# Attention and a mixture of experts: GpSimd makes the low parts of the next rows, ScalarE scales a block's last half

## The chip, the cores and the metric

The program runs on one core of one Trainium2 chip. Its time is the device time of one execution in microseconds (us); lower is better. The times of the kernel before are those of three runs, with their median; one more execution was profiled. Engines are named as the profile names them: PE is TensorE, DVE is VectorE, ACT is ScalarE, POOL is GpSimd, SP is SyncE, which here issues transfers.

## What is computed

Attention with pooled keys and values gives x; then each token goes through one expert, picked by a gate that may keep the expert of the token before.

```python
attn = softmax(q @ mean8(k).T / sqrt(64)); x = attn @ mean8(v)      # B 8, H 8, S 576, head 64
logits = x @ w_gate                                                   # 8 experts
e[s]   = argmax(logits[s]) if s == 0 or sigmoid(x[s] @ w_local) < 0.5 else e[s-1]
out[s] = softmax(logits[s])[e[s]] * (relu(x[s] @ w1[e[s]]) @ w2[e[s]])    # 512 -> 1024 -> 512
```

## The kernel before, in words

Up to some 200 us the program computes the attention, routes the 4608 tokens and lists them by expert; that part is written as a plan of steps and is not touched here. What follows works on *blocks* of 256 listed rows (two halves of 128) that share one expert. The first blocks are in the plan; the rest is a loop at line 1197 over a table that the kernel itself has computed. With these inputs the loop makes 19 passes, one block each. A pass with two halves is a *full block*; a pass with one half only (`l1_one`) is a *single-half pass*.

Every product is made of three products of parts: a number is cut into a high part (rounded to the matmul's type, a copy on ACT) and a low part (the number less its high part, a subtract, on DVE). So x has `xt[:, :, 0]` and `xt[:, :, 1]`, the weights have `w1h` and `w1l`, `w2h` and `w2l`, the hidden values `ht_h` and `ht_l`.

One pass runs so, engine by engine in the order in which the code stands (the schedule is by hand; each engine keeps the order of the code and waits on semaphores):

- `head`: DVE takes the row numbers of the block after the next (`m_d`, `idk`); POOL gathers these rows from DRAM into `xg` (`fetch`, L1098 and L1099, then two indirect transfers, L299).
- Layer 1: in a full block eight block columns, each of four pairs of matmuls L322 and L324 (one pair for each quarter of the 512 inputs: `w1h` by both parts of x, then `w1l` by the high part) into one of six PSUM tiles. ACT copies a piece out (L329), DVE adds (L330), ACT makes `ht_h` (L334) and DVE `ht_l` (L335). In between DVE transposes the next block's rows, which SP had written out and read back in pieces (L303, L307), into `xs` (L310). A single-half pass has its own form (L976 to L991), in which DVE transposes all rows at once (L982) before it makes `ht_l` (L991).
- Layer 2 of half 1 (`l2(1)`, full blocks only). A half's layer 2 is 24 matmuls L346.
- `rest`: SP writes `xg` out and reads it back turned. If the next block has another expert (`chg > 0`, in six passes), ACT casts the four quarters of the loaded `raw1` to `w1h` (L172) and DVE subtracts for `w1l` (L173). DVE shifts the row numbers (`meta_shift`, L1165). Half 1 of the output is scaled by the gate (`emit_scale(1)`, L1078, DVE, from PSUM) and POOL scatters it to the output's rows (`emit_rows`, L1087 to L1089). `next_rows` cuts the next block's x into parts: two ACT casts (L315), two DVE subtracts (L316), each for two quarters. Then `l2(0)` on PE, the new `w2h` and `w2l` (L177, L178) where the expert changes, the scale of half 0 on DVE and its scatter on POOL. `seen_o` writes one number into a half of `ob` so that the next scale is ordered behind the scatter.

`ob`, `zf`, `m_e` and `m_a` are small tables and the output buffer of a block; `o_ps` are its two PSUM tiles, 2348 for half 1 and 2347 for half 0 in the listings below. Line 1243 is the end of the program, with barriers.

Of the kernel before, what the change touches and what calls it, by code (L numbers as in the profile page):

```python
# [8 lines left out]
F32 = mybir.dt.float32  # L9
F32R = mybir.dt.float32r  # L10
I32 = mybir.dt.int32
AF = mybir.ActivationFunctionType
ALU = mybir.AluOpType
# [92 lines left out]
def moe_attention(ctx: ExitStack, tc: tile.TileContext, q, q_st, k, v, v_st, w_gate, w1, w2, out):  # L106
    nc = tc.nc
# [133 lines left out]
    m_a = route.tile([P, 2, 2], F32, name="m_a", bufs=1)  # L241
# [39 lines left out]
    def rows_split(c2, tp, xt):  # L281
        cs = slice(2 * c2, 2 * c2 + 2)
        tv = tp.rearrange("p (c n) -> p c n", c=2)
        nc.scalar.copy(out=xt[:, cs, 0, :], in_=tv)
        nc.vector.tensor_tensor(out=xt[:, cs, 1, :], in0=tv, in1=xt[:, cs, 0, :].bitcast(F32), op=ALU.subtract)
# [5 lines left out]
    def row_numbers(out, m):  # L291
        nc.vector.tensor_copy(out=out, in_=m[:, :, 0])  # L292
# [9 lines left out]
    def rows_pieces():  # L302
        nc.sync.dma_start(xd.rearrange("(h p) d -> p h d", h=2), xg)  # L303

    def pieces_rows():
        for r in range(4):
            nc.sync.dma_start(xq[r * QP:(r + 1) * QP], xd[:, r * P:(r + 1) * P].rearrange("(m t) j -> t m j", t=QP))  # L307
# [4 lines left out]
    def next_rows():  # L312
        for c2 in range(2):
            cs = slice(2 * c2, 2 * c2 + 2)
            nc.scalar.copy(out=xt[:, cs, 0, :], in_=xs[:, cs, :])  # L315
            nc.vector.tensor_tensor(out=xt[:, cs, 1, :], in0=xs[:, cs, :], in1=xt[:, cs, 0, :].bitcast(F32), op=ALU.subtract)  # L316

    TERMS = ((0, 0), (0, 1), (1, 0))

# [18 lines left out]
    def l2(h, kks=range(KF), to=None):  # L338
        to = to or o_ps
        if len(kks) == 1:  # L340
            jobs = [(kk, i, j) for kk in kks for (i, j) in TERMS]
        else:
            jobs = [(kk, i, j) for k0 in range(0, KF, 4) for i in range(2) for kk in range(k0, k0 + 4) for j in range(2 - i)]
        n = 3 * kks[0]
        for (kk, i, j) in jobs:
            nc.tensor.matmul(out=to[h], lhsT=ht[i][:, kk, h * P:(h + 1) * P], rhs=W2[j][:, kk, :],  # L346
                             start=(n == 0), stop=(n == 3 * KF - 1))
            n += 1

    with ExitStack() as actx:  # L350
# [419 lines left out]
        def do(name, n):  # L770
# [136 lines left out]
            elif op == "i2":  # L907
                ids_load(bass.ds(entry(2, 1, (EN.SP,), NU32 - TB), TB))
            elif op == "ld":
                n0 = entry(0, 3, (EN.SP,), E - 1)  # L910
                load1(rw1, n0)
                load2(rl2, n0)
            elif op in ("e0", "e1"):
                h = int(op[1])
                emit_scale(h)
                if not h:
                    seen_o(1)
                apart(emit_rows(h))
            elif op == "f0":
                rows_meta(m_b, NS)  # L920
            elif op == "f1":
                ids_take(m_c)
                row_numbers(idf, m_c)
            elif op == "f2":
                xg = ld.tile([P, 2, D], F32, name="vt_in", bufs=3)
                xq = ld.tile([P, TB, P], F32, name="vt_in", bufs=3)
                xs = ld.tile([P, KD, 2 * P], F32, name="vt_in", bufs=3)
                xgs["f"] = ld.tile([P, 2, D], F32, name="qt", bufs=4)
                gather(xgs["f"], idf)
            elif op == "i3":  # L930
                ids_load(bass.ds(entry(3, 1, (EN.SP,), NU32 - TB), TB))
            else:
                raise ValueError(name)
# [10 lines left out]
        ob = sp.tile([P, 2, D], F32, name="ob")  # L944
# [14 lines left out]
        o_ps = [pp.tile([P, D], F32, name=f"o_ps{i}") for i in range(2)]  # L959
# [114 lines left out]
            nc.sync.dma_start(tab.rearrange("o (j c) -> o j c", c=TI), tabc[0:TROWS, :])  # L1074
            yield

        def emit_scale(h):
            nc.vector.tensor_scalar(out=ob[:, h, :], in0=o_ps[h], scalar1=m_a[:, h, 1:2], scalar2=None, op0=ALU.mult)  # L1078

        def seen_o(h):  # L1080
            nc.gpsimd.tensor_tensor(out=ob[:, h, 0:1], in0=zf1, in1=zf1, op=ALU.add)  # L1081
# [4 lines left out]
        def emit_rows(h):  # L1086
            nc.gpsimd.tensor_tensor(out=m_e[h], in0=m_i[:, h:h + 1], in1=zi, op=ALU.add)  # L1087
            nc.gpsimd.tensor_tensor(out=zf2[:, h:h + 1], in0=m_e[h].bitcast(F32), in1=ob[:, h, 0:1], op=ALU.mult)  # L1088
            return nc.gpsimd.indirect_dma_start(out=outv, out_offset=bass.IndirectOffsetOnAxis(ap=m_e[h][:, 0:1], axis=0),  # L1089
                                                in_=ob[:, h, :], in_offset=None, bounds_check=NT - 1, oob_is_err=False)  # L1090

        def meta_shift():
            nc.vector.tensor_copy(out=m_a, in_=m_b)
            row_numbers(m_i, m_b)
            nc.vector.tensor_copy(out=m_b, in_=m_c)
# [35 lines left out]
    def weights1(chg, nx):  # L1131
        for c in range(KD):
            split1(rw1(c), c, nc.vector)
        with tc.If(chg > 1):
            load1(rw1, nx)

    def weights2(chg, nx):
        for c in range(KF // 2):
            split2(rw2(c), c, nc.vector)
        with tc.If(chg > 1):  # L1140
            load2(rl2, nx)

    def changes(j):
        return entry(j + 1, 2, (EN.Activation, EN.DVE, EN.SP), 2), entry(j + 1, 3, (EN.SP,), E - 1)

    def first(chg, nx):
        with tc.If(chg > 0):
            weights1(chg, nx)
# [10 lines left out]
    def rest(j, turned=False):  # L1159
        rows_pieces()  # L1160
        pieces_rows()
        chg, nx = changes(j)
        first(chg, nx)
        meta_shift()
        nc.vector.tensor_copy(out=m_c, in_=m_d)  # L1165
        if turned:
            for c2 in range(2):
                rows_split(c2, hp[3 + c2], xt)
        seen_o(0)
        emit_scale(1)  # L1170
        first_half = emit_rows(1)
        if not turned:
            next_rows()
        l2(0)
        with tc.If(chg > 0):  # L1175
            weights2(chg, nx)
        emit_scale(0)
        tc.declare_no_dep(emit_rows(0).ins, first_half.ins, reason="rows of a block are distinct")
        seen_o(1)

# [11 lines left out]
    for c2 in range(2):  # L1192
        rows_turn(c2, xgs["f"], hp[3 + c2])
    rest(1, turned=True)
    trips = entry(0, 4, ALLE, NB2)
    man.close()
    with tc.For_i(2, trips, 1, iteration_sync="reg_based", name="blocks") as iv:  # L1197
        with tc.manual_schedule():
            two = entry(iv, 0, (EN.PE, EN.Activation, EN.DVE), 1)
            head(iv)  # L1200
            with tc.If(two > 0) as both:
                two_halves()
            with both.Else():
                l1_one()
            rest(iv)
# [41 lines left out]
```

## Time and profile before

| what | value |
|---|---|
| median of three runs | 626.25 us (622.35, 626.25, 628.47) |
| profiled execution | 623.03 us, span 621.3 us |
| PE busy, share of the span | 594.5 us, 96% |
| DVE / ACT / POOL busy | 439.7 / 291.8 / 273.6 us |
| mean granted clock of TensorE | 0.991 |
| transfers, share of 16 engines' span, SP's queue / POOL's queue | 43.5% / 11.0% |

The span runs from the first to the last instruction; the run's time is 1.7 us longer. Busy shares are means over the attention, the loop and the end, which have different limits, so the rows further down are read by stretch. Ends of matmuls are modelled, and spans on POOL are rough.

### The profile page before, as it was taken

The numbers are of one execution on the slowest core, as the hardware profiler recorded it, in microseconds if no ns is written. First come the engines' busy times: TensorE is split into PE (matmuls) and PEld (weight loads), VectorE is DVE, ScalarE is ACT, GpSimd is POOL, SyncE is SP. The second block draws the span as 40 slices with busy tenths as digits, with TensorE's granted clock in tenths as the row PEclk, the third lists the DMA queues.
The fourth block names the chain that finished last, engine by engine and source line by source line (L and its number), as shares of the span: only waits on it lengthen the run. The fifth ranks groups of instructions, "written<-read, shape, count | busy, mean of one in ns | idle before, by whom it ended". The sixth has DMA issues, their size and how long they took to land. (4 is left out here: it accounts for less than half of the span.)

```text
span 621.3 us, 14355 instructions
## 1 busy us (share of the span) xinstructions
PE 594.5 (96%) x3386; PEld 509.3 (82%) x3387; DVE 439.7 (71%) x1035; ACT 291.8 (47%) x697; POOL 273.6 (44%) x505
## 2 busy tenths in 40 slices
PE   8999999999999999999999999999999999999991
PEld 7898988898878878888887877787888888888870
DVE  7899898999766426565885686889556686654781
ACT  2777777965433313242742373746233363422550
POOL 6686776776673425134134326132352213341242
PEclk9999999999999999999999999999999999999996
DMA  8998973975003584331663486577543385322403
GB/s 340 356 383 303 365 276 103 318 173 204 19 2 102 176 301 135 102 118 68 211 228 113 143 259 219 186 242 267 196 127 105 101 258 195 115 71 85 118 27 99
DMA packets 62009, 111.95 MB, mean 180 GB/s; under 512 B 13466, under 2 KB 33946, under 8 KB 61980
## 3 DMA queue, kind: packets, MB, share of 16 engines
q1 hardware_dynamic: 53468, 89.54, 43.5%
q0 software_dynamic: 8512, 22.07, 11.0%
q8 instruction: 13, 0.21, 0.1%
q14 instruction: 16, 0.13, 0.1%
HBM read 81.88 MB, written 31.80 MB: 183 GB/s over the span
## 5 line engine op out<-in xcount | busy, mean ns | idle before, releaser
L322 PE MATMUL hp<-x,w1h 128*128 128x512 f32 x364 | 130.7, 400 | 2.5 <-DVE x L316 2.5
L346 PE MATMUL o_ps<-w2h,ht_h 128*128 128x512 f32 x312 | 122.8, 393 | 1.2 <-ACT ht_h L990 1.2
L346 PE MATMUL o_ps<-w2l,ht_h 128*128 128x512 f32 x312 | 122.1, 391 | 0.4 <-DVE w2l L178 0.2
L324 PE MATMUL hp<-x,w1l 128*128 128x256 f32 x364 | 102.2, 281 | 0.0
L329 ACT COPY hs<-hp 128x256 f32<-128x256 f32 x91 | 33.4, 369 | 125.8 <-PE hp L324 120.5
L346 PE MATMUL o_ps<-w2h,ht_l 128*128 128x512 f32 x312 | 87.8, 391 | 1.4 <-DVE ht_l L991 1.4
L322 PEld LDWEIGHTS hp<-x,w1h 128*128 128x128 f32 x364 | 68.4, 188 | 20.4 <-issue 3.8
L334 ACT ACTIVATE ht_h<-hs 128x256 fp32r<-128x256 f32 x136 | 57.1, 420 | 37.5 <-DVE hs L330 30.4
L1087 POOL TENSOR_TENSOR m_e<-m_i,zi 128x1 int32<-128x1 int32 x42 | 8.5, 201 | 142.3 <-DVE m_i L292 136.4
L346 PEld LDWEIGHTS o_ps<-w2h,ht_h 128*128 128x128 f32 x312 | 58.6, 188 | 14.6 <-issue 2.2
L346 PEld LDWEIGHTS o_ps<-w2h,ht_l 128*128 128x128 f32 x312 | 58.4, 188 | 14.5 <-DVE ht_l L991 2.2
L1078 DVE TENSOR_SCALAR ob<-o_ps,m_a 128x512 f32<-128x512 f32 x42 | 31.5, 750 | 53.9 <-PE o_ps L346 50.6
L324 PEld LDWEIGHTS hp<-x,w1l 128*128 128x128 f32 x364 | 68.9, 189 | 0.7
L346 PEld LDWEIGHTS o_ps<-w2l,ht_h 128*128 128x128 f32 x312 | 58.7, 188 | 12.5 <-DVE w2l L178 1.3
L565 PE MATMUL op<-vaug,aT 128*128 128x148 f32 (+4 forms) x448 | 66.0, 306 | 0.7 <-ACT osb L367 0.6
L565 PEld LDWEIGHTS op<-vaug,aT 128*128 128x128 f32 (+1 forms) x448 | 60.0, 179 | 3.9 <-issue 1.3
L335 DVE SCALAR_TENSOR_TENSOR ht_l<-hs,ht_h 128x256 fp32r<-128x256 f32 x136 | 56.4, 416 | 5.9 <-ACT ht_h L334 5.5
L1088 POOL TENSOR_TENSOR zf<-m_e,ob 128x1 f32<-128x1 f32 x42 | 13.9, 331 | 96.1 <-DVE ob L1078 65.2
L1089 POOL DMA_INDIRECT out<-ob,m_e x42 | 45.8, 1091 | 18.8 <-issue 18.8
L330 DVE TENSOR_TENSOR hs<-hp,hs 128x256 f32<-128x256 f32 x91 | 37.3, 417 | 19.9 <-ACT hs L329 11.5
L704 POOL DMA_INDIRECT ids<-pm,pos x36 | 38.7, 1076 | 17.0 <-DVE pos L699 8.0
L299 POOL DMA_INDIRECT vt_in<-x_rows,idk x40 | 39.8, 995 | 10.1 <-issue 8.1
(256 smaller groups left out, 1170.2 us busy)
## 6 DMA issues: line engine op xcount, KB each, us to landing
raw<-in_moe_w SPq DMA_DIRECT2D x48, 512.0 KB
xd<-vt_in SPq DMA_DIRECT2D x20, 512.0 KB
vt_in<-xd SPq DMA_DIRECT2D x80, 128.0 KB
kk<-in_k SPq DMA_DIRECT2D x16, 576.0 KB
qt<-in_q SPq DMA_DIRECT2D x16, 512.0 KB
vt_in<-in_v SPq DMA_DIRECT2D x16, 512.0 KB
x_rows<-xs SPq DMA_DIRECT2D x16, 512.0 KB
vt_in<-in_v_st SPq DMA_DIRECT2D x8, 256.0 KB
```

Source lines behind the costliest of these rows:

```text
L299: nc.gpsimd.indirect_dma_start(out=xg[:, h, :], out_offset=None, in_=x_rows[0:NT + 1], in_offset=bass.IndirectOffsetOnAxis(ap=idk[:, h:h + ...
L322: nc.tensor.matmul(out=ps, lhsT=W1[0][:, kk, f * P:(f + 1) * P], rhs=xt[:, kk].rearrange("p i n -> p (i n)"), start=(kk == 0), stop=False, ...
L324: nc.tensor.matmul(out=ps[:, 0:2 * P], lhsT=W1[1][:, kk, f * P:(f + 1) * P], rhs=xt[:, kk, 0, :], start=False, stop=(kk == KD - 1), skip_g ...
L329: nc.scalar.copy(out=hb[:, 0, :], in_=ps[:, 2 * P:])
L330: nc.vector.tensor_tensor(out=hb[:, 1, :], in0=ps[:, 0:2 * P], in1=hb[:, 0, :], op=ALU.add)
L334: nc.scalar.activation(out=ht[0][:, f, :], in_=hb, func=AF.Relu)
L335: nc.vector.scalar_tensor_tensor(out=ht[1][:, f, :], in0=hb, scalar=0.0, in1=ht[0][:, f, :].bitcast(F32), op0=ALU.max, op1=ALU.subtract)
L346: nc.tensor.matmul(out=to[h], lhsT=ht[i][:, kk, h * P:(h + 1) * P], rhs=W2[j][:, kk, :], start=(n == 0), stop=(n == 3 * KF - 1))
L565: nc.tensor.matmul(out=out, lhsT=lhs, rhs=rhs if len(out.shape) == 3 else rhs.rearrange("p s x -> p (s x)"), start=all(x[0] != n for x in ...
L704: ins = nc.gpsimd.indirect_dma_start(out=ids.rearrange("t m w -> (t m) w"), out_offset=bass.IndirectOffsetOnAxis(ap=pos[:, u:u + 1], axis= ...
L1078: nc.vector.tensor_scalar(out=ob[:, h, :], in0=o_ps[h], scalar1=m_a[:, h, 1:2], scalar2=None, op0=ALU.mult)
L1089: return nc.gpsimd.indirect_dma_start(out=outv, out_offset=bass.IndirectOffsetOnAxis(ap=m_e[h][:, 0:1], axis=0), in_=ob[:, h, :], in_offse ...
```

## The change

Two edits, both in what `rest` issues. The low parts of the next rows (L316) are made by POOL instead of DVE, in each call of `next_rows`; and `next_rows` is called earlier, ahead of `meta_shift` and of the first scatter's work on POOL. The scale of half 0 is made by ACT (an activation that copies with a scale), behind the `w2h` casts, instead of by DVE; the scale of half 1 stays on DVE, and so do both scales of the first block, in the plan. The block ahead of the loop (`turned`) takes its x by another way and changes only in its last scale. Lines from 1078 on stand 1 to 3 lower in the kernel after.

```diff
--- before.py
+++ after.py
@@ -313,7 +313,7 @@
         for c2 in range(2):
             cs = slice(2 * c2, 2 * c2 + 2)
             nc.scalar.copy(out=xt[:, cs, 0, :], in_=xs[:, cs, :])
-            nc.vector.tensor_tensor(out=xt[:, cs, 1, :], in0=xs[:, cs, :], in1=xt[:, cs, 0, :].bitcast(F32), op=ALU.subtract)
+            nc.gpsimd.tensor_tensor(out=xt[:, cs, 1, :], in0=xs[:, cs, :], in1=xt[:, cs, 0, :].bitcast(F32), op=ALU.subtract)
 
     TERMS = ((0, 0), (0, 1), (1, 0))
 
@@ -1074,7 +1074,10 @@
             nc.sync.dma_start(tab.rearrange("o (j c) -> o j c", c=TI), tabc[0:TROWS, :])
             yield
 
-        def emit_scale(h):
+        def emit_scale(h, late=False):
+            if late:
+                nc.scalar.activation(out=ob[:, h, :], in_=o_ps[h], func=AF.Copy, scale=m_a[:, h, 1:2])
+                return
             nc.vector.tensor_scalar(out=ob[:, h, :], in0=o_ps[h], scalar1=m_a[:, h, 1:2], scalar2=None, op0=ALU.mult)
 
         def seen_o(h):
@@ -1161,6 +1164,8 @@
         pieces_rows()
         chg, nx = changes(j)
         first(chg, nx)
+        if not turned:
+            next_rows()
         meta_shift()
         nc.vector.tensor_copy(out=m_c, in_=m_d)
         if turned:
@@ -1169,12 +1174,10 @@
         seen_o(0)
         emit_scale(1)
         first_half = emit_rows(1)
-        if not turned:
-            next_rows()
         l2(0)
         with tc.If(chg > 0):
             weights2(chg, nx)
-        emit_scale(0)
+        emit_scale(0, late=True)
         tc.declare_no_dep(emit_rows(0).ins, first_half.ins, reason="rows of a block are distinct")
         seen_o(1)
```

POOL, in the loop, from the gathers of a pass on, before (`vt_in` is `xg`, `x_2506` is `xt`, `zf_2335` is `zf1`; a row is an instruction's line, operation, out<-in and shape):

```order
L299 DMA vt_in<-x_rows,idk 128x512 x2
L1081 TENSOR_TENSOR ob<-zf_2335 128x1
L1147 UNCONDITIONAL_BRANCH
L1087 REGISTER_ALU
L1087 TENSOR_TENSOR m_e_2332<-m_i,zi 128x1
L1088 ISA
L1088 TENSOR_TENSOR zf_2337<-m_e_2332,ob 128x1
L1089 DMA out<-ob,m_e_2332 4608x512
```

and after:

```order
L299 DMA vt_in<-x_rows,idk 128x512 x2
L1150 UNCONDITIONAL_BRANCH
L316 TENSOR_TENSOR x_2506<-vt_in,x_2506 128x2x256
L1178 UNCONDITIONAL_BRANCH
L316 ISA
L316 TENSOR_TENSOR x_2506<-vt_in,x_2506 128x2x256
L1084 TENSOR_TENSOR ob<-zf_2335 128x1
L1090 REGISTER_ALU
L1090 TENSOR_TENSOR m_e_2332<-m_i,zi 128x1
L1091 ISA
L1091 TENSOR_TENSOR zf_2337<-m_e_2332,ob 128x1
L1092 DMA out<-ob,m_e_2332 4608x512
```

Two subtracts of 128x2x256 now stand between the gathers and everything that belongs to the scatters; `seen_o(0)` (`ob<-zf_2335`) has moved behind them.

DVE at the same place, from the last copy of the row numbers to the first subtracts of `w2l`, before:

```order
L1165 COPY m_c<-m_d 128x4
L1078 REGISTER_ALU
L1078 TENSOR_SCALAR ob<-o_ps_2348,m_a 128x512
L316 REGISTER_ALU
L316 TENSOR_TENSOR x_2506<-vt_in,x_2506 128x2x256
L316 REGISTER_ALU
L316 TENSOR_TENSOR x_2506<-vt_in,x_2506 128x2x256
L1175 COMPARE_AND_BRANCH
L178 ISA
L178 TENSOR_TENSOR w2l<-raw_2937,w2h 128x1024
```

and after:

```order
L1170 COPY m_c<-m_d 128x4
L1081 REGISTER_ALU
L1081 TENSOR_SCALAR ob<-o_ps_2348,m_a 128x512
L1178 COMPARE_AND_BRANCH
L178 ISA
L178 TENSOR_TENSOR w2l<-raw_2937,w2h 128x1024
```

Between the scale of half 1 and the subtracts of `w2l` nothing is left.

ACT from its last `w2h` cast to the end of a pass, before:

```order
L177 CAST w2h<-raw_2937 128x1024
L1140 COMPARE_AND_BRANCH
L1140 UNCONDITIONAL_BRANCH
L1175 REGISTER_ALU
L1175 UNCONDITIONAL_BRANCH
L1140 UNCONDITIONAL_BRANCH
L1197 ISA
L1197 COMPARE_AND_BRANCH
L1197 UNCONDITIONAL_BRANCH
```

and after:

```order
L177 CAST w2h<-raw_2937 128x1024
L1143 COMPARE_AND_BRANCH
L1143 UNCONDITIONAL_BRANCH
L1178 REGISTER_ALU
L1178 UNCONDITIONAL_BRANCH
L1143 UNCONDITIONAL_BRANCH
L1079 ISA
L1079 ACTIVATE ob<-o_ps_2347,m_a 128x512
L1200 ISA x2
L1200 COMPARE_AND_BRANCH
L1200 UNCONDITIONAL_BRANCH
```

The scale of half 0 is now ACT's last operation of a pass, ahead of the branch to the next. On DVE the operation L1078 at that place is gone.

## Rows read from the trace of the kernel before

**Rows 1.** Page, first line: span of the profiled execution.

```profile
span 621.3 us, 14355 instructions
```

**Rows 2.** Busy time by stage, most of the loop; engines with instruction counts.

```profile
core 0: us, PE busy (x) PEld busy (x) DVE busy (x) ACT busy (x) POOL busy (x), PEclk, DMA share, GB/s
409.00:608.00 199.00, 196.42 (x971) 163.91 (x969) 134.27 (x286) 83.86 (x180) 64.71 (x138) 1.00 0.44 143
```

**Rows 3.** Waits of PE, 215 to 621 us: in total, times, longest.

```profile
PE hp L322 <- DVE x L316: 2.5, 2, 1.3
PE o_ps L346 <- DVE ht_l L991: 1.4, 2, 0.7
```

**Rows 4.** Timeline 392 to 407 us: start, length, engine, line, [idle before].

```profile
394.16 3.90 ACT L172 CAST w1h<-raw 128x1024 fp32r<-128x1024 f32 x4 [1.36 <-PE o_ps L346]
...
395.44 4.63 DVE L173 TENSOR_TENSOR w1l<-raw,w1h 128x1024 fp32r<-128x1024 f32 x4 [2.18 <-ACT w1h L172]
...
397.96 1.14 ACT L315 CAST x<-vt_in 128x512 fp32r<-128x512 f32 x2
...
401.42 1.28 DVE L316 TENSOR_TENSOR x<-vt_in,x 128x512 fp32r<-128x512 f32 x2
...
402.25 0.47 PE L322 MATMUL hp<-x,w1h 128*128 128x512 f32 x1 [1.11 <-DVE x L316]
...
404.06 0.37 ACT L329 COPY hs<-hp 128x256 f32<-128x256 f32 x1 [1.17 <-PE hp L324]
...
405.44 0.37 ACT L329 COPY hs<-hp 128x256 f32<-128x256 f32 x1 [1.01 <-PE hp L324]
```

**Rows 5.** Groups by line and shape: xcount | busy us, mean ns | idle before.

```profile
L603 POOL TENSOR_TENSOR xs<-osb,rr 128x512 f32<-128x512 f32 x26 | 26.9, 1051 | 13.6 <-DVE vaug L441 4.4 <-ACT aT L367 2.4 <-DMA kt<-in_moe_w 2.3
...
L178 POOL TENSOR_TENSOR w2l<-vt_in,w2h 128x1024 fp32r<-128x1024 f32 x2 | 4.7, 2372 | 1.8 <-ACT w2h L177 1.8
...
L316 DVE TENSOR_TENSOR x<-vt_in,x 128x512 fp32r<-128x512 f32 x38 | 24.4, 683 | 0.0
...
L172 ACT CAST w1h<-raw 128x1024 fp32r<-128x1024 f32 x24 | 23.4, 1048 | 7.7 <-PE o_ps L346 7.7
...
L879 ACT ACTIVATE ob<-o_ps,idm 128x512 f32<-128x512 f32 x2 | 1.4, 684 | 1.8 <-PE o_ps L346 1.8
```

**Rows 6.** Timeline of POOL and DVE at three other places, same columns.

```profile
119.60 2.37 POOL L178 TENSOR_TENSOR w2l<-vt_in,w2h 128x1024 fp32r<-128x1024 f32 x1
...
120.26 2.81 DVE L173 TENSOR_TENSOR w1l<-kt,w1h 128x1024 fp32r<-128x1024 f32 x1
...
143.44 2.05 POOL L603 TENSOR_TENSOR xs<-osb,rr 128x512 f32<-128x512 f32 x2
143.49 2.05 DVE L582 TENSOR_SCALAR rr<-osb 128x16 f32<-128x16 f32 x1
...
401.65 0.50 POOL L1088 TENSOR_TENSOR zf<-m_e,ob 128x1 f32<-128x1 f32 x1 [1.16 <-DVE ob L1078]
```

**Rows 7.** Timeline of the last pass, 599 to 605 us.

```profile
599.18 0.74 DVE L1078 TENSOR_SCALAR ob<-o_ps,m_a 128x512 f32<-128x512 f32 x1
...
601.39 2.03 DVE L982 STREAM_TRANSPOSE vt_in<-vt_in 128x1024 f32<-128x1024 f32 x1 [0.91 <-ACT ht_h L990]
...
604.04 1.21 PE L346 MATMUL o_ps<-w2h,ht_l 128*128 128x512 f32 x4 [0.68 <-DVE ht_l L991]
```

**Rows 8.** Timeline of DVE at 388 us.

```profile
387.75 0.64 DVE L310 STREAM_TRANSPOSE vt_in<-vt_in 128x256 f32<-128x256 f32 x1 [1.92 <-DMA vt_in<-xd]
```

**Rows 9.** Timeline of the end: POOL's last gather, SP's queue.

```profile
604.57 0.96 POOL L299 DMA_INDIRECT vt_in<-x_rows,idk  x1 [0.30 <-issue]
...
609.28 0.40 SPq L303 DMA_DIRECT2D xd<-vt_in  x1
```

**Rows 10.** Waits of SP's queue, 600 to 621 us: in total, times, longest.

```profile
SPq L303 <- DMA vt_in<-x_rows,idk: 7.3, 1, 7.3
```

**Rows 11.** Line L1243: ns min/median/max, first and last start in us.

```profile
L1243 POOLq DRAIN  x5: 40/88/6936, 611.6 to 621.0; - x5
```

## The prediction

> **What bounds the kernel now.** The program runs on one core; the loop, some 380 us of the 621.3 us span [rows 1], is where both edits work. Read the stages first: from 409 to 608 us PE is busy 196.4 of 199 us, DVE 134 and POOL 65, and the granted clock is 1.00, the upper level of 2.4 GHz [rows 2]. So the loop is bound by PE, and an engine beside it matters only where PE waits. The list of PE's waits is therefore the next view: 2.5 us in two waits for the low parts of x (L316), longest 1.3, and 1.4 us in two waits for `ht_l` (L991), 0.7 each [rows 3]. That is all that this change can take from PE's waits; a larger gain must come from the end.
>
> The third view is the timeline at one of the two L316 waits [rows 4]. This pass loads new weights. The reader should follow DVE: four subtracts of `w1l` end at 395.44+4.63=400.07, then come the small copies and the scale of half 1, then the two L316 from 401.42. PE, held 1.11 us, starts at 402.25. ScalarE's copies of x had ended at 397.96+1.14=399.10: x waits for its turn on DVE, not for data.
>
> **The change part by part.**
>
> *Low parts to GpSimd.* DVE loses two subtracts of 683 ns per pass, 38 in 19 passes [rows 5]; back to back a pair takes 1.28 us [rows 4]. POOL gains two. POOL has done no such subtract of 128x512 before. Nearest rows: a multiply of this size at 1.05 us, and a subtract of twice the size into the same type at 2.37 us, half of which is 1.19 [rows 5]. I take 1.19, the same operation; the bounds are 1.05 and, if half the size saved nothing, 2.37.
>
> *What POOL's subtract does to DVE.* A subtract with both inputs in SBUF on DVE took 2.81 us beside POOL's 2.37 us one: POOL ended at 119.60+2.37=121.97 and DVE at 123.07, 1.10 later, which is about the length of the subtract (4.63/4=1.16 [rows 4]). So DVE stood until POOL was through. Two POOL operations back to back held a tiny DVE operation for 2.05 us, both of them [rows 6]. The other way round, POOL's `zf` of one column took 0.50 us, to just past the end of the first L316 at 402.1: POOL waits for the running DVE instruction, then goes first.
>
> In a pass with new weights that sets these times (origin as in [rows 4]): the first x copy ends about 398.6 (0.62 each); DVE's third subtract ends about 395.44+3x1.16=398.9; POOL's two run from 398.9 to 401.3; DVE's fourth subtract runs from there to 402.4. PE could start at 402.25-1.11=401.14. It needs the first half of x (400.1), the second half half a block column later (a column takes 405.44-404.06=1.38 us [rows 4], so about 401.8; ready 401.3), and the last quarter of `w1l` at about three quarters, 402.2 to 402.4. So x no longer holds PE, and the fourth `w1l` just does or just doesn't: 0.1 us is left here and, as the second place was held 0.24 longer, about 0.4 there. **Gain 2.5-0.5=2.0 us.**
>
> The Trainium skill, "SBUF — State Buffer", section "Who interferes with whom", has this as a lock that is held for one instruction, the second to issue blocking fully. By that rule DVE's fourth subtract would run between POOL's two, the second half of x would come at about 402.4, and each place would keep about 0.6 us: a gain of 1.3 instead of 2.0. The pair at 143.44 speaks for the longer hold.
>
> DVE's chain in such a pass: +2.3 (fourth subtract), -1.2 (no L316), so its `w2l` subtracts end 1.1 later.
>
> *Scale of half 0 to ScalarE.* DVE loses 0.74 us [rows 7], pitch 0.67. ScalarE did this operation elsewhere in 684 ns [rows 5]. It stands behind the four `w2h` copies, or waits for PE's last matmul where there are none; behind it wait the next pass's branch and first L329, which in a full block feed six PSUM tiles, so PE doesn't need them for several columns: hidden. Where weights are new, the scale no longer waits for the `w2l` subtracts, so the second scatter, and POOL's whole row of work for the next pass, comes earlier. Where they are not, PE's end still sets it. Net on DVE: 1.1-0.67=+0.4 us per pass with new weights (six: 24 casts, four each [rows 5]).
>
> That +0.4 falls on the two L991 waits, in single-half passes after new weights: `ht_l` comes behind scale, copies and transpose (599.18, 601.39), and PE waits 0.68 for it [rows 7]. One of the two is the last pass, where SP's queue ends the program (below). **Loss 0.4 us.** The bound the other way is 0.7 gained, if the lock costs DVE nothing.
>
> The same +0.4, with PE about 1.1 earlier, could make the block of the second place late in its own ReLUs. Against that works DVE's wait of 1.92 us for the turned rows at 387.75 [rows 8]: those rows come from gathers that POOL issues behind the second scatter, now about 1.4 us earlier. I leave it at zero; it is worth up to 1.2 us either way.
>
> *Added waits.* The matmuls now wait for POOL and DVE apart, with four register operations more in a full block. Every such wait in layer 2 has one now, and no gap there appears among PE's waits [rows 3]: nothing. On POOL the subtracts wait for ScalarE's copies; behind them stand `seen_o`, `m_e`, `zf` and both scatters. The first scatter comes about 2 us later in such a pass; nobody in the loop waits for it but the next scale of that half, a pass away. Where no weights are new, the subtracts run under layer 2 of PE, 11 us in a full block.
>
> *The end.* SP's queue waits for the last gathers [rows 10] (issued at 604.57 [rows 9]), writes `xd` at 609.28, and walks the rest of its program to the end. In the last pass, after new weights, the gather stood behind the second scatter, which stood behind DVE's late scale at 599.18; now `idk` on DVE sets it, about 1.5 us earlier. Bounds: 2.7 gained without the lock; or 1.1 lost, if POOL's drain of 6.94 us [rows 11] follows POOL's last scatter at a fixed distance, since that scatter comes about 1.1 later behind the subtracts. I take **1.0 gained**.
>
> **Sum.** -2.0+0.4-1.0=-2.6 us. The profiled execution took 623.03 us, so 620.4 by it; the median shown is 626.25 (622.35 to 628.47), so **623.6** against that, which I forecast.
>
> **Rivals.**
> *No gain (same).* The fourth `w1l` takes the place of L316 as the last thing that PE waits for, DVE's +0.4 is felt at every place, and POOL's drain keeps the end. For it: the last pieces miss or meet PE by 0.1 to 0.4 us by my own times. 626.3, within 1.2.
> *More gain.* POOL's pair slips between DVE's instructions at no cost. Then both L316 waits go (2.5), the L991 wait too (0.7), and the end gives 2.3: 626.25-5.5=620.8. Against it: [rows 6].
> *Slower.* One mechanism: POOL's subtract is slow and holds DVE's fourth `w1l`. It loses once a subtract takes over 1.7 us (PE needs that quarter by 402.3 and waited until 402.25+1.0=403.3 for it before; 398.9+2x1.7+1.1=403.4). At 2.37 us it ends at 404.7, 1.4 late in six passes (8), plus 2.8 at one L991: about 11 more, 637. The Trainium skill, "GPSIMD Engine Reference", section "Engine selection", makes GpSimd about twice as slow as VectorE for two inputs; as an estimate from 683 ns that is 1.37 us a subtract, below the point, and would take 0.7 us from the gain.
>
> **How the numbers follow.** Forecast (1 to 4 us less) 0.55; no gain 0.28; more gain 0.10; slower by the lock 0.07. About 1% (6 us) is what a measurement of this kernel tells from no change, as its three runs spread over 6 us. No case but the slow one leaves that band, and that only in its upper half; the runs' own spread gives some chance to each side: faster 0.06, same 0.88, slower 0.06. The range takes the spread of the runs around the cases: low 622.35-4=618.4, high 628.5, the highest run at no gain; the forecast's own is 622 to 625 at the shown median.
>
> **What would show it.** Right: no wait of PE for x; L316 on POOL near 1.2 us; in passes with new weights one DVE subtract near 3.4 us (1.1 plus two POOL subtracts); `ob` on ScalarE near 0.68 us; SP's `xd` about 1.5 us sooner after the last matmul. Wrong: PE waiting for L316 on POOL or L173; a POOL subtract over 1.7 us; POOL's drain moving with its last scatter; any change before 215 us.

## The result, and the profile after

| | before | after |
|---|---|---|
| median of 20 runs each | 625.14 us | 627.51 us |
| ratio, 95% interval | | 1.0057 (1.0038 to 1.0077) |
| span of the profiled execution | 621.3 us | 628.6 us |

By the ratio the change costs about 3.6 us, where a gain of 2.6 had been forecast. A second measurement of the same changed kernel gave 1.0062 (1.0037 to 1.0087).

The spans of the two profiled executions are 7.3 us apart, twice what the ratio gives. Part of that lies ahead of everything that was changed: PE's last matmul ahead of the loop starts at 227.56 in the profile before, at 230.62 in the one after, and at 226.92 in the second profile of the changed kernel. So all profiles below are compared **from that matmul on**: to PE's last matmul ("loop"), and from there to the end of the span ("end"). By this, 393.7 us before and 398.0 and 397.7 after: 4.2 and 4.0 more, which agrees with the ratio.

The list of PE's waits in the profile after, from 215 us on (in total, times, longest), which answers to [rows 3]:

```profile
PE o_ps L346 <- DVE ht_l L991: 2.4, 2, 1.5
PE hp L322 <- POOL ob L1084: 1.6, 2, 1.3
PE hp L976 <- POOLq L1200: 0.8, 1, 0.8
PE hp L976 <- ACTq L1200: 0.7, 1, 0.7
PE hp L322 <- issue: 0.7, 1, 0.7
```

The two waits for L316 on DVE are gone. But the waits for `ht_l` have grown from 1.4 to 2.4, and there are three kinds of wait that the kernel before doesn't have: two for something on POOL (named `ob L1084`, POOL's instruction right behind the second L316), one on POOL's branch into the loop (L1200), one that the list calls "issue". (The wait on ACT's branch is not new: in the kernel before it stood on DVE's, 0.7 us too.) One by one:

**The loop's entry.** Timeline of the first loop pass, PE and POOL (start, length, engine, line, [idle before]); then the busy times and the granted clock of the stretch (third figure from the right):

```profile
231.75 0.47 PE L976 MATMUL hp<-w1h,x 128*128 128x512 f32 x1 [0.74 <-ACTq L1200]
231.93 0.19 POOL L1091 TENSOR_TENSOR zf<-m_e,ob 128x1 f32<-128x1 f32 x1 [1.81 <-ACT ob L1079]
232.06 0.40 PE L976 MATMUL hp<-w1l,x 128*128 128x512 f32 x1
233.28 0.70 PE L976 MATMUL hp<-w1h,x 128*128 128x512 f32 x2 [0.82 <-POOLq L1200]
```

```profile
core 0: us, PE busy (x) PEld busy (x) DVE busy (x) ACT busy (x) POOL busy (x), PEclk, DMA share, GB/s
231.00:241.00 10.00, 8.40 (x32) 6.41 (x32) 2.35 (x3) 2.13 (x5) 4.14 (x9) 0.83 0.47 132
```

The third matmul is the first that reads a low part of x. It starts 1.22 us after the second, instead of 0.23. This low part was made ahead of the loop, by DVE (`rows_split`, which the change leaves alone), and POOL's first L316 starts only at 243.2 us (last listing of this section): PE waits here for no result of POOL. The wait that later passes need is part of the loop's code, and in the first pass it ends when POOL has come into the loop. POOL is still at the last scatter of the block ahead, which waits for that block's scale. Behind the stall the granted clock fell to its lower level (0.50 from 234.2 to 237.2 us), and nine matmuls started up to 0.43 us apart instead of 0.23, 1.6 us in all. Together 2.6 us.

**A pass with new weights.** The same kind of rows at the second place of [rows 3] (the subtracts one at a time):

```profile
428.48 1.14 ACT L315 CAST x<-vt_in 128x512 fp32r<-128x512 f32 x2
429.23 1.38 POOL L316 TENSOR_TENSOR x<-vt_in,x 128x512 fp32r<-128x512 f32 x1 [7.28 <-PE o_ps L346]
429.37 2.32 DVE L173 TENSOR_TENSOR w1l<-raw,w1h 128x1024 fp32r<-128x1024 f32 x1
430.57 2.25 POOL L316 TENSOR_TENSOR x<-vt_in,x 128x512 fp32r<-128x512 f32 x1
431.62 1.23 DVE L1096 COPY m_a<-m_b 128x4 f32<-128x4 f32 x1
433.07 0.47 PE L322 MATMUL hp<-x,w1h 128*128 128x512 f32 x1 [1.30 <-POOL ob L1084]
```

Read the ends: POOL 430.61, DVE 431.69, POOL 432.82, DVE 432.85. The two engines take turns. DVE's fourth `w1l` stands until POOL's first subtract is through, then runs its 1.1; POOL's second stands until `w1l` is through, then runs its 1.1; a copy of four columns, 0.17 us elsewhere, stands 1.23 us until that is through. PE gets the second half of x 1.5 us late.

**A single-half pass.** At 380 to 387 us:

```profile
380.67 1.14 ACT L315 CAST x<-vt_in 128x512 fp32r<-128x512 f32 x2 [2.56 <-DVE vt_in L982]
382.03 0.99 POOL L299 DMA_INDIRECT vt_in<-x_rows,idk  x1 [0.29 <-issue]
383.33 0.96 POOL L299 DMA_INDIRECT vt_in<-x_rows,idk  x1 [0.30 <-issue]
384.31 2.52 POOL L316 TENSOR_TENSOR x<-vt_in,x 128x512 fp32r<-128x512 f32 x2
385.81 0.47 PE L322 MATMUL hp<-x,w1h 128*128 128x512 f32 x1 [0.68 <-issue]
387.08 0.47 PE L322 MATMUL hp<-x,w1h 128*128 128x512 f32 x1 [0.34 <-POOL ob L1084]
```

ACT's high parts end at 381.81. POOL takes them up at 384.31, right behind its two gathers, and PE loses 1.35 us in two pieces.

**The end.** POOL's last scatter, and the drain that ends POOL's program (ns min/median/max, first and last start), which answers to [rows 11]:

```profile
618.28 1.01 POOL L1092 DMA_INDIRECT out<-ob,m_e  x1 [0.57 <-issue]
```

```profile
L1246 POOLq DRAIN  x5: 40/88/7817, 618.6 to 628.3; - x5
```

PE's last matmul starts at 613.97, so the last scatter comes 4.31 us behind it; before it was 2.59. The drain ends at 618.59+7.82=626.41, 8.13 behind that scatter's start (8.34 before), and the span 2.2 later.

The lengths themselves came near the forecast: ACT's scale of half 0 takes 686 ns in the mean of 20, L316 on POOL this (ns min/median/max):

```profile
L316 POOL TENSOR_TENSOR x<-vt_in,x x38: 1287/1294/2279, 243.2 to 612.6; 128x512 fp32r<-128x512 f32 x38
```

### The profile page after: what moved, and what is told of

It is laid out like the page before. It is cut to its first block, busy times and chain, and to the rows that moved or that the text cites. A ratio compares the mean times of both kernels' runs of the same rounds, so it can differ in the third digit from the quotient of the medians.

```text
span 628.6 us, 14562 instructions
## 1 busy us (share of the span) xinstructions
PE 596.0 (95%) x3386; PEld 510.2 (81%) x3387; DVE 445.1 (71%) x977; ACT 304.4 (48%) x717; POOL 331.2 (53%) x543
## 5 line engine op out<-in xcount | busy, mean ns | idle before, releaser
L316 POOL TENSOR_TENSOR x<-vt_in,x 128x512 fp32r<-128x512 f32 x38 | 54.7, 1460 | 116.3 <-PE o_ps L346 83.1
L330 DVE TENSOR_TENSOR hs<-hp,hs 128x256 f32<-128x256 f32 x91 | 37.3, 417 | 42.4 <-ACT hs L329 36.6
L1092 POOL DMA_INDIRECT out<-ob,m_e x42 | 47.7, 1136 | 19.6 <-issue 18.7
L1079 ACT ACTIVATE ob<-o_ps,m_a 128x512 f32<-128x512 f32 x20 | 13.7, 686 | 77.7 <-PE hp L322 52.4
L322 PE MATMUL tp<-x,w1h 128*128 128x512 f32 x120 | 43.0, 398 | 0.0
```

Source lines behind the costliest of these rows:

```text
L316: nc.gpsimd.tensor_tensor(out=xt[:, cs, 1, :], in0=xs[:, cs, :], in1=xt[:, cs, 0, :].bitcast(F32), op=ALU.subtract)
L322: nc.tensor.matmul(out=ps, lhsT=W1[0][:, kk, f * P:(f + 1) * P], rhs=xt[:, kk].rearrange("p i n -> p (i n)"), start=(kk == 0), stop=False, ...
L330: nc.vector.tensor_tensor(out=hb[:, 1, :], in0=ps[:, 0:2 * P], in1=hb[:, 0, :], op=ALU.add)
```

## The experiments

All in one table; each ratio is to runs of the kernel before in the same series, and columns 3 to 5 come from each kernel's profile, counted as above. "Scatter" is the start of POOL's last scatter, after the start of PE's last matmul and ahead of the end of the span.

| kernel | ratio to before (95%) | loop, us | end, us | sum | scatter: after / ahead |
|---|---|---|---|---|---|
| before | 1 | 380.06 | 13.68 | 393.7 | 2.59 / 11.08 |
| after | 1.0057 (1.0038, 1.0077) | 383.35 | 14.60 | 398.0 | 4.31 / 10.30 |
| after, again | 1.0062 (1.0037, 1.0087) | 383.16 | 14.58 | 397.7 | 4.29 / 10.29 |
| scale alone | 0.9945 (0.9922, 0.9968) | 377.13 | 12.45 | 389.6 | 2.15 / 10.30 |
| low parts alone | 1.0104 (1.0078, 1.0130) | 384.25 | 15.16 | 399.4 | 4.86 / 10.30 |
| early, on DVE | 0.9989 (0.9963, 1.0014) | 377.85 | 14.08 | 391.9 | 3.06 / 11.03 |
| on POOL, old place | 1.0722 (1.0689, 1.0755) | 429.66 | 13.84 | 443.5 | 3.54 / 10.30 |
| split in halves | 1.0003 (0.9974, 1.0031) | 380.11 | 13.94 | 394.1 | 3.63 / 10.31 |
| idle subtracts | 1.0220 (1.0181, 1.0260) | 394.21 | 13.84 | 408.1 | 3.53 / 10.31 |
| on POOL, ahead of w1h | 1.0025 (0.9992, 1.0057) | 381.47 | 14.60 | 396.1 | 4.31 / 10.29 |
| on DVE, ahead of w1h | 0.9959 (0.9935, 0.9983) | 378.17 | 13.33 | 391.5 | 3.03 / 10.30 |
| both scales on ACT | 0.9894 (0.9863, 0.9925) | 374.77 | 12.48 | 387.3 | 2.18 / 10.30 |

The sums, each of one profile, follow the ratios to about 1 us (for the one on POOL in the old place: 50 us by the sum, 45 by the ratio). So the waits of these profiles can be set against the differences in time.

The theories: **A**, the loss comes from GpSimd's subtracts (PE's wait for POOL at the loop's entry, POOL and DVE holding each other, POOL's queue). **B**, it comes from ScalarE's late scale. **C**, the place costs. **D**, only the waits for POOL's results cost, not the holding of DVE.

### Each edit alone

Scale alone: the subtracts go back to DVE and to their old place.

```diff
-            nc.gpsimd.tensor_tensor(out=xt[:, cs, 1, :], ...
+            nc.vector.tensor_tensor(out=xt[:, cs, 1, :], ...
-        if not turned:
-            next_rows()
         meta_shift()
...
         first_half = emit_rows(1)
+        if not turned:
+            next_rows()
```

> The second edit alone: ScalarE scales half 0 behind its copies of w2h; low parts stay on DVE in their old place. Theory A (what was lost lies in GpSimd's subtracts: PE waits at the loop's entry for POOL, POOL and DVE hold each other in turn, the subtracts queue behind gathers): no stall between the second and the third matmul of the first loop pass (1.0 us in the changed kernel), granted clock of 1.0 there; PE's waits for L316 on DVE stay near 2.5 us in two; the two waits for ht_l (L991, 1.4 us) shrink to under 0.4, since DVE has 0.67 less to do; time 0.5 to 2.5 us below before (ratio 0.996 to 0.999). Theory B (ScalarE's late scale is the cause: it enters the loop later, and PE after it): the stall and the lower clock at the entry are here too, ratio 1.003 or more.

Low parts alone:

```diff
-        emit_scale(0, late=True)
+        emit_scale(0)
```

> The first edit alone: GpSimd makes the low parts, ahead of the first scatter; DVE keeps the scale of half 0. Theory A: the entry's stall of 1.0 us and the granted clock below 1.0 behind it are here (2.6 us together); in passes with new weights DVE's fourth w1l takes 2.3 us and POOL's second subtract 2.3 us; the waits for ht_l (L991) are longer than the changed kernel's (2.4 us in two), near 3.5; ratio to before 1.006 to 1.011. Theory B: no stall at the entry, ratio 1.000 or less.

PE's waits but for the one of 0.7 on ACT's or DVE's branch at the loop's entry, of the scale alone, then of the low parts alone (there without five of 0.2 to 0.7 us in sum):

```profile
PE hp L322 <- DVE x L316: 2.0, 2, 1.5
```

```profile
PE o_ps L346 <- DVE ht_l L991: 3.6, 2, 1.9
PE hp L322 <- POOL ob L1084: 1.7, 2, 1.3
PE hp L976 <- POOLq L1200: 0.9, 1, 0.9
```

The scale alone makes the kernel faster, by 3.4 us (0.55%); the low parts alone make it slower by 6.5. B falls: the stall at the entry is where POOL makes the low parts and not where only ACT has the scale. The scale alone was worth more than was expected of it: both waits for `ht_l` are gone (1.7 us from start to start), and the last scatter comes 0.4 sooner after PE's end, after which nothing else holds the end up (12.45 instead of 13.68). The low parts then take it all back. In the low parts alone the same stall at the entry stood without a lower clock behind it.

### The place

Early, on DVE:

```diff
-            nc.gpsimd.tensor_tensor(out=xt[:, cs, 1, :], ...
+            nc.vector.tensor_tensor(out=xt[:, cs, 1, :], ...
```

> The changed kernel with the subtracts back on DVE, in the new, earlier place. Theory A: no stall at the entry, no wait of PE for x over 0.3 us (DVE's two subtracts end 1.3 us after the fourth w1l, ahead of the small copies and the scale), waits for ht_l under 0.7 us in sum, the last scatter about 2.2 us after PE's last matmul instead of 3.9 and the end with it: 3 to 5 us below before, ratio 0.992 to 0.996. Theory B: as the changed kernel, ratio 1.003 or more. Theory C (the earlier place itself costs, since the small copies, the scale and the first scatter come 1.3 us later): ratio 1.000 to 1.004.

On POOL, in the old place:

```diff
-        if not turned:
-            next_rows()
         meta_shift()
...
         first_half = emit_rows(1)
+        if not turned:
+            next_rows()
```

> The changed kernel with POOL's subtracts in the old place, behind the first scatter. Theory A: the entry's stall and lower clock stay (2.6 us); in passes with new weights the subtracts now also wait for the scale and the scatter's issue, so PE waits for L316 on POOL 1 to 4 us at two or more places; ratio to before 1.008 to 1.016, slower than the changed kernel. Theory C (the place costs): faster than the changed kernel, ratio under 1.004. The end: last scatter about 2 to 3 us after PE's last matmul, and the span ends a fixed 11 us after that scatter.

The first brought 0.7 us where 3 to 5 were expected. DVE's two subtracts still stand behind four `w1l`, and these ended 2.0 and 1.5 us later in their passes than with the scale alone, so that PE still waited 1.3 and 0.6 us for x (from start to start). For the first of the two places the rows show why. The scale of half 1 stands behind the subtracts, so the two scatters near 365 us start 1.6 and 1.1 us later (after the same matmul) than with the scale alone; POOL waits 2.83 us for a scatter to land, its next gathers start 4.3 us later, and DVE stands for the turned rows of the next block:

```profile
388.79 0.63 DVE L310 STREAM_TRANSPOSE vt_in<-vt_in 128x256 f32<-128x256 f32 x1 [4.10 <-DMA vt_in<-xd]
```

With the scale alone it stood 2.09 us there. The last scatter came 0.9 later than with the scale alone, so that the gain at the end was lost as well. The early place on DVE is worse than the old one by 0.4% (0.9989 against 0.9945, the intervals just overlap): theory C holds for it. Of the 2.3 us between their sums 1.6 are at the end; in the loop PE waits 0.4 less for x and 0.8 for `ht_h`, which is new.

The second lost 45 us by the ratio, and only the direction was expected. PE's three largest waits:

```profile
PE hp L322 <- issue: 19.9, 8, 3.8
PE hp L976 <- POOL x L316: 6.5, 2, 3.3
PE hp L322 <- POOL m_e L1090: 5.3, 8, 1.3
```

In the old place POOL's subtracts stand behind the first scatter, which waits for the scale of half 1, which waits for PE's layer 2 of half 1. Only layer 2 of half 0 is left to cover them, and it is too short in ten passes, not in the two or three with new weights that were thought of. From start to start PE waited 35 us for x; about 15 more went into matmuls behind the longer of these waits, which ran at the lower clock (0.51 from 428 to 435 us). With GpSimd, the earlier place is needed.

### Which of the three costs

Split in halves: DVE makes the low part of the first two quarters, POOL that of the last two.

```diff
-            nc.gpsimd.tensor_tensor(out=xt[:, cs, 1, :], ...
+            (nc.vector, nc.gpsimd)[c2].tensor_tensor(out=xt[:, cs, 1, :], ...
```

> The changed kernel with the low part of the first two quarters of x on DVE and only that of the last two on POOL, both in the new place. Theory A (three costs of POOL's subtracts: PE's wait for POOL at the loop's entry, DVE and POOL holding each other, the queue behind the gathers): the first loop pass reads POOL's half six matmuls (1.4 us) later, so the entry's stall of 1.0 us falls under 0.3; POOL holds DVE once a pass with new weights instead of twice, so the waits for ht_l are 0.3 to 1.5 us in sum instead of 2.4; DVE's one subtract stands behind the fourth w1l, PE's waits for x 1.5 to 3 us in sum; ratio to before 0.997 to 1.003. Rival D (any use of POOL for x costs the whole): stall of 1.0 at the entry, ratio 1.004 to 1.008.

PE's waits, but for the one on ACT at the entry:

```profile
PE hp L322 <- DVE m_i L292: 2.4, 2, 1.5
PE o_ps L346 <- DVE ht_l L991: 1.3, 2, 0.8
...
PE hp L322 <- POOL m_e L1090: 0.7, 1, 0.7
```

The stall at the entry is gone, since PE needs POOL's half six matmuls later. The waits for `ht_l` fell between those of the two kernels (1.6 from start to start; before 1.7, after 2.7, scale alone none). For x PE waited 3.5 in all, a little more than expected.

Idle subtracts: the scale alone, and POOL makes the same two subtracts again into a buffer that nobody reads. This adds work and leaves nothing out.

```diff
+    scr = [rawp.tile([P, 2, 2 * P], F32R, name=f"scr{i}") for i in range(2)]
...
+    def high_rows():
+        for c2 in range(2):
+            cs = slice(2 * c2, 2 * c2 + 2)
+            nc.scalar.copy(out=xt[:, cs, 0, :], in_=xs[:, cs, :])
+            nc.gpsimd.tensor_tensor(out=scr[c2], in0=xs[:, cs, :], in1=xt[:, cs, 0, :].bitcast(F32), op=ALU.subtract)
...
         first(chg, nx)
+        if not turned:
+            high_rows()
         meta_shift()
```

> The kernel with the second edit alone (ScalarE's scale), and POOL besides makes the same two subtracts in the new place into a buffer that nobody reads; DVE still makes the ones that PE reads, in the old place. This adds work and leaves none out. Theory A: the work itself holds DVE though nobody waits for its result: in passes with new weights the fourth w1l takes 2.3 us and the first small copy 1.2, PE's waits for L316 on DVE rise from 2.0 to 5 to 8 us in sum, those for ht_l from 0 to 1 to 3 us, POOL's last scatter comes 1 to 2 us later after PE's last matmul; no stall at the loop's entry, since PE reads nothing of POOL's; ratio to before 1.003 to 1.012. Rival D (only the waits for POOL's result cost): as the kernel without these subtracts, ratio 0.993 to 0.997.

PE's two largest waits (L321 is DVE's subtract for x here), then POOL and DVE in a pass without new weights:

```profile
PE hp L327 <- DVE x L321: 10.7, 8, 2.6
PE hp L981 <- DVE x L321: 3.3, 2, 1.8
```

```profile
235.94 2.53 POOL L316 TENSOR_TENSOR scr<-vt_in,x 128x512 fp32r<-128x512 f32 x2 [1.41 <-ACT x L315]
...
235.98 1.28 DVE L1101 COPY m_a<-m_b 128x4 f32<-128x4 f32 x1 [0.46 <-DVEq L1156]
237.17 0.15 DVE L292 CAST m_i<-m_b 128x2 int32<-128x2 f32 x1
237.36 1.14 DVE L1103 COPY m_b<-m_c 128x4 f32<-128x4 f32 x1
```

Nobody waits for these two subtracts, and yet the kernel is 2.8% slower than without them (1.0220 against 0.9945, 17 us). D falls: the work itself holds DVE. In each of the 19 passes one or two of the small copies (the cast `m_i` among them) take 0.8 us or more; with the scale alone all take 0.16 to 0.17. POOL's queue is not what holds DVE: its scale follows the last copy by 0.13 us in the pass shown, as it does at this place with the scale alone. The rows show how: `m_a` begins 0.04 us after POOL's first subtract and lasts until it is through, `m_i` slips in between the two, `m_b` begins beside the second and lasts until it is through. DVE's subtracts for x then come late: PE waited 14.0 us for them, in ten passes, and some 2 us more went into matmuls at the lower clock behind two of these waits. More was lost than expected, since I had looked at passes with new weights only.

On POOL, ahead of w1h: the changed kernel with `next_rows` ahead of `first`, where DVE is idle.

```diff
-        first(chg, nx)
         if not turned:
             next_rows()
+        first(chg, nx)
         meta_shift()
```

> The changed kernel with the casts of x and POOL's subtracts one step earlier still, ahead of the casts of w1h. DVE sits idle there for about 2.3 us, until the first w1h. Theory A: POOL's pair lies in that idle time, DVE's four w1l take 4.6 to 5.0 us instead of 5.7, no wait of PE for x over 0.3 us in passes with new weights, waits for ht_l under 0.8 in sum; the stall at the entry stays, and the wait behind the gathers in the single-half pass near 380 us may stay (1.3 us); ratio to before 0.998 to 1.004, below the changed kernel by 2 to 4 us. Rival D (the lock is not the cause; POOL's own lateness is): as the changed kernel, ratio 1.004 to 1.008.

Timeline of POOL and DVE in a pass with new weights, then in the single-half pass near 380 us, then two of PE's waits:

```profile
397.23 2.57 POOL L316 TENSOR_TENSOR x<-vt_in,x 128x512 fp32r<-128x512 f32 x2 [7.49 <-PE o_ps L346]
...
399.88 4.63 DVE L173 TENSOR_TENSOR w1l<-raw,w1h 128x1024 fp32r<-128x1024 f32 x4 [3.71 <-PE o_ps L346]
...
378.28 0.96 POOL L299 DMA_INDIRECT vt_in<-x_rows,idk  x1 [0.31 <-PE o_ps L346]
379.26 2.50 POOL L316 TENSOR_TENSOR x<-vt_in,x 128x512 fp32r<-128x512 f32 x2
```

```profile
PE hp L322 <- issue: 1.8, 1, 1.8
...
PE hp L976 <- POOLq L1200: 0.9, 1, 0.9
```

With the pair moved out of DVE's way the four `w1l` take 4.63 us again instead of 5.74, and PE waits for x in no pass with new weights. The other two costs stay: the stall at the entry (1.0), and in the single-half pass the subtracts behind the gathers (2.5 us from start to start, and behind it 1.1 us more at a granted clock of 0.50). About half of the change's loss is won back (1.0025 against 1.0057; the intervals overlap, so the size is not sure). The waits for `ht_l` stayed larger (1.4 from start to start) than expected; I did not follow why.

### Two versions without GpSimd

On DVE, ahead of w1h: the same place, `nc.vector` in L316, ScalarE's late scale.

> The same place, ahead of the casts of w1h, but the subtracts on DVE, and ScalarE's late scale. Theory A: DVE makes them in its idle 2.3 us; no wait of PE for x over 0.3 us, none for ht_l, no stall at the entry; the last scatter some 3 us after PE's last matmul, as with the early place on DVE (2.1 with ScalarE's scale alone); 3 to 6 us below before, ratio 0.990 to 0.996. Theory C (moving the casts ahead delays w1h and w1l by their 1.1 us, and PE waits for w1l instead): ratio 0.997 to 1.002.

PE's waits, without that on ACT at the entry:

```profile
PE o_ps L346 <- ACT ht_h L334: 1.2, 3, 0.6
PE o_ps L346 <- DVE ht_l L991: 0.8, 2, 0.4
```

No wait for x is left, and yet the loop takes 1.0 us more than with the scale alone. PE, no longer held at x, now waits at the end of layer 1 for ACT's ReLUs, which wait for DVE's L330 between its transposes L310. DVE is not behind with its work there; it stands for the turned rows:

```profile
387.72 0.63 DVE L310 STREAM_TRANSPOSE vt_in<-vt_in 128x256 f32<-128x256 f32 x1 [5.11 <-DMA vt_in<-xd]
```

With the scale alone that was 2.09 us. As with the early place on DVE, POOL had waited for a scatter to land (3.24 us), and the gathers of these rows start 4.5 us later than with the scale alone.

Both scales on ACT: low parts on DVE behind the four `w1l`, the small copies ahead of the weights, and both of the loop's scales on ScalarE.

```diff
-        first(chg, nx)
-        if not turned:
-            next_rows()
         meta_shift()
         nc.vector.tensor_copy(out=m_c, in_=m_d)
+        first(chg, nx)
+        if not turned:
+            next_rows()
...
-        emit_scale(1)
+        emit_scale(1, late=not turned)
```

> Low parts back on DVE behind its four w1l, the small copies of the row numbers ahead of the weights (DVE idles there), and both scales in the loop on ScalarE. Against the kernel with ScalarE's late scale alone DVE has 0.75 us less per pass and 1.4 us less between w1l and the end of x's low parts. Theory A: PE's waits for x fall from 2.0 to under 1.0 in sum, none for ht_l, no stall at the entry, the last scatter 2 to 3 us after PE's last matmul; ratio to before 0.990 to 0.996, at or below the second edit alone (0.9945). Theory F (ScalarE becomes late instead: its scale of half 1 stands between the casts of x and of w2h, and puts w2h and w2l 0.7 later): waits of PE for w2l or for the ReLUs of the next block, 1 to 2 us, ratio 0.996 to 1.000.

All of PE's waits from 215 us on, and DVE in a pass with new weights:

```profile
PE hp L976 <- ACTq L1200: 0.7, 1, 0.7
```

```profile
390.39 4.63 DVE L173 TENSOR_TENSOR w1l<-raw,w1h 128x1024 fp32r<-128x1024 f32 x4 [0.52 <-ACT w1h L172]
394.94 1.33 DVE L316 TENSOR_TENSOR x<-vt_in,x 128x512 fp32r<-128x512 f32 x2
396.19 4.62 DVE L178 TENSOR_TENSOR w2l<-raw,w2h 128x1024 fp32r<-128x1024 f32 x4
```

The ratio of 0.9894 (medians 615.29 and 622.76 us) is the only one below that of the scale alone, though the two intervals just overlap; its sum is 2.3 us lower. Between the last `w1l` and the first `w2l` DVE does nothing but x, and PE waits for nothing in the loop but its entry. ACT has the time: in the kernel before it was busy for 291.8 of 621.3 us.

### The changed kernel again

> The changed kernel once more, unchanged, for a second profile: the stall at the loop's entry (1.0 us), the waits for ht_l (2.4 to 2.7 in two), the wait behind the gathers near 380 us and the last scatter 4.3 us after PE's last matmul are there again; the lower granted clock behind the entry's stall, which of five profiles with that stall only one showed, is expected to be absent. Ratio 1.003 to 1.008.

PE's three largest waits:

```profile
PE o_ps L346 <- DVE ht_l L991: 2.3, 2, 1.4
PE hp L322 <- POOL ob L1084: 2.1, 3, 1.3
PE hp L976 <- POOLq L1200: 1.3, 1, 1.3
```

They are the same waits at the same places as in the first profile; the wait behind the gathers was 1.8 us from start to start instead of 1.35. The stall at the entry was 1.5 us this time, and the clock stayed at its upper level behind it. So the lower clock of the first profile is not a part of the change that every execution pays: of the five profiles with this stall (after twice, low parts alone, on POOL in the old place, on POOL ahead of w1h) one has it. (Before this run there were four such profiles, not five as its expectation says.)

## Why the prediction was wrong

Three steps of the prediction failed. It put the loop's entry at nothing; it did not ask what stands ahead of the subtracts in POOL's queue; and it took a gain at the end where POOL's last scatter, now later, sets the end. A fourth, the hold of DVE by POOL, was taken for the whole pair of subtracts, and the gain of 2.0 at x that was worked out from it came to 1.3 and 0.7. The terms of the forecast's sum, and what they measured in the two profiles of the changed kernel (us against before; distances of matmul starts beyond those of the same matmuls where nothing is waited for):

| term | forecast | first | second |
|---|---|---|---|
| the two L316 waits, new weights | -2.0 | -1.3 | -0.7 |
| x behind POOL's gathers | none | +1.35 | +1.8 |
| the loop's entry | 0 | +2.6 | +1.5 |
| `ht_l` (L991) | +0.4 | +1.0 | +0.9 |
| five short waits for `ht_h` in single-half passes | none | -0.5 | -0.5 |
| the end | -1.0 | +0.9 | +0.9 |
| sum | -2.6 | +4.1 | +3.9 |

Point by point:

- **The durations were nearly right.** L316 on POOL was put at 1.19 and took 1.29 (median); ACT's scale was put at 0.684 and took 0.686, hidden as forecast. The rival in which the sum turns at 1.7 us a subtract had the right engine pair and the wrong cause: the kernel became slower with subtracts far below that point.
- **The hold.** The prediction took it that DVE stands until POOL's pair is through, from [rows 6]. The traces show turns, one instruction each. DVE loses about what was forecast (1.1 on `w1l` and 1.1 on the first small copy), but x comes later: its second half behind DVE's fourth `w1l`, not ahead of it. The Trainium skill, "SBUF — State Buffer", section "Who interferes with whom", says that whoever issues first has the shared ports for its whole instruction while the other blocks; the prediction set this beside the rows and worked it out (1.3 gained instead of 2.0), and chose the rows. The measured 1.3 and 0.7 are on the page's side. The DVE operation that "stood for both" in [rows 6] does not decide it: the runs show that one can come in between (the fourth `w1l` above), not that it must, and why that one did not stays open.
- **The queue.** The prediction asked what is queued *behind* POOL's subtracts and never what is queued *ahead* of them. In a single-half pass after new weights that is two gathers of a microsecond each, themselves late behind a scatter. DVE's queue has nothing of the kind there. This is read from the rows, and from the wait's absence where DVE makes these parts early or in the old place; it was not tried apart from the rest.
- **The loop's entry.** This is the step "Added waits ... nothing". It looked at layer 2 of later passes. But an operand that POOL makes in the loop also ties PE to the moment when POOL enters the loop, and POOL enters last, behind the scatter of the block ahead. That is settled: the stall is in all five profiles in which POOL makes the low parts of the first two quarters, and in none of the others, the split in halves among them. A wait of this kind stood in the list of the kernel before, in a line that [rows 3] leaves out:

```profile
PE hp L976 <- DVEq L1197: 0.7, 1, 0.7
```

- **The two edits were netted against each other.** On DVE +1.1 and -0.67 gave +0.4, and the waits for `ht_l` were charged with that. Apart, they are far from small: the scale alone takes these waits to nothing and the end down by 1.2, the low parts alone take the waits to 3.9 from start to start and the end up by 1.5.
- **The end.** The bound on the side of a loss (1.1) was the right one, and close: the drain moves with POOL's last scatter. In ten of the twelve profiles the span ends 10.29 to 10.31 us after that scatter's start; in the other two (before; early on DVE) it is 11.0 to 11.1. In those two SP's queue comes last, as the prediction had it for the kernel before: its drain starts 0.6 and 0.7 us after POOL's has ended; in the changed kernel it starts before that. With POOL's two subtracts ahead of both scatters in the last pass, where DVE's small copies are held as well, the scatter came 1.7 us later. SP's write of the rows was sooner after the last matmul, as forecast, but by 0.7 and not 1.5, and it no longer decides.
- **What the first place did.** There PE didn't wait for x at all in the first profile: ACT's casts of `w1h` began sooner in their pass, since DVE's wait for the turned rows [rows 8] was 1.01 instead of 1.92. The forecast named this effect and left it at zero.

But for 0.4 us at `ht_l`, the forecast called none of its uncertain steps on the side of a loss, and nearly all fell there. Its 0.88 for no clear change rested on the spread of the runs and not on the mechanism. Its signs of being wrong were the right ones to look at: PE waiting for L316 on POOL, and POOL's drain moving with its last scatter, are both in the trace.

## What to carry to other kernels

An engine that takes over an operand of the bound engine brings its whole queue into that operand's path: look at what stands ahead of it in each kind of pass, and at the first pass of a loop, not only at the length of the operation. Work given to GpSimd was not free for VectorE even where nobody read the result, while the scales given to ScalarE added no wait of PE (the second of them was tried only together with two moves in DVE's order): with two engines to choose from, try the work on both. And two edits with opposite signs are costed, and if possible timed, apart; here one was worth -3.4 us and the other +6.5 to 7.

## What the runs showed of the hardware

- DVE and POOL, both with operands in SBUF, took turns instruction by instruction: a DVE copy of 128x4 that takes 0.17 us alone took 1.28 beside a POOL subtract of 128x512 and 1.23 at another place, and a POOL subtract that takes 1.29 took 2.25 behind a DVE subtract of 128x1024.
- After a stall of PE of 1.0 to 1.5 us at the loop's entry the granted clock fell to its lower level in one profile of five. It fell behind some longer waits as well (0.50 behind one of 2.5 us, 382.1 to 385.4 us of the kernel with POOL ahead of w1h), so that a wait of PE can cost more than its length: about 15 us beside 35 with POOL in the old place.
- The end of the program stood 10.29 to 10.31 us behind the start of POOL's last scatter in ten profiles, over sums from 387 to 444 us; in the two others, where SP's queue came last, at 11.0 to 11.1.
